# Four of six weight tiles in steps 2 to 8 of a chunk, two in an earlier pass, and a changed order of two loads

## The chip, the cores and the metric

The kernel runs on one core of a Trainium2 chip. The metric is the device time of one execution in microseconds, beginning to end. A core has TensorE (matmuls; PE in the profile, with its weight loads as PEld), VectorE (DVE), ScalarE (ACT), GpSimd (POOL) and SyncE (SP), which here issues every DMA. Each engine takes its instructions strictly in the order of the program; between engines, semaphores tell when data is there and when a buffer is free. SyncE too works in order: a DMA that has to wait holds up all DMAs behind it.

## What is computed

Two equal layers on an input of 2048 rows by 512 columns. Each adds a Fourier mixing and then an MLP block:

```python
def _A_ref(x, dft_seq_re, dft_seq_im, dft_hid_re, dft_hid_im):
    a = jnp.einsum("bsd,ed->bse", x, dft_hid_re)
    b = jnp.einsum("bsd,ed->bse", x, dft_hid_im)
    return jnp.einsum("ts,bse->bte", dft_seq_re, a) - jnp.einsum("ts,bse->bte", dft_seq_im, b)

def _B_ref(x, w1, w2, w3, w4):
    h = _gelu(_layernorm(x) @ w1)
    ...                                # h in four groups, shifted by +1, -1, +2, -2 rows
    x1 = x + hs @ w2
    return x1 + _gelu(_layernorm(x1) @ w3) @ w4

for _ in range(2):
    x = x + _A_ref(_layernorm(x), ...)
    x = x + _B_ref(_layernorm(x), ...)
```

w3 is 512 by 1376 and w4 1376 by 512. The same weights serve both layers.

## The kernel before

**Products in three parts.** Every f32 operand is split into a high part, rounded to the matmul's format, and a low part, the rest. A product is three matmuls (`mm3`, lines 301 to 303): high by high, high by low, low by high. The high part is a copy on ScalarE, the low part a subtraction on VectorE. Weights that come from HBM go through `raw` buffers and a ring of four blocks: line 247 writes a block's high half, line 264 its low half. The third matmul of an `mm3` group is the first that reads the low half of the left operand.

**The MLP by chunks.** The 2048 rows are four chunks of 512. The inner size of 1376 is cut into NF = 11 tiles of 128 (the last is padded). In layer 0, chunks 0 and 1 form the *first pair*, worked off by `by_pairs`; chunks 2 and 3 go one after the other through `mlp`. In layer 1 both pairs go through `by_pairs`, and the second of them is `last_pair`.

*`mlp`* runs 13 steps a chunk. Step t multiplies by tile t of w3 (12 matmuls, t < 11), takes the gelu (ScalarE, line 661) and splits it (VectorE, lines 667 and 664), and multiplies tile t - 2 by w4 (12 matmuls, t > 1). So steps 0, 1, 11 and 12 have 12 matmuls and the others 24. At its begin, step t prepares the low half of the ring block for step t + 2 and the high half of the one for t + 3. After each step the main loop (lines 1601 to 1621) adds other work for VectorE and ScalarE: in chunk 2 the w4 sums, in steps 9 and 10 the split of chunk 3's input (`rt_split`, lines 625 and 626), and from step 6 on, for the next layer's first product, the pieces called `xp`: statistics (line 315), normalisation (line 349), sums (lines 381 to 383), their high parts (lines 386 to 390) and low parts (line 401), for one pair of row tiles after another.

*`by_pairs`* multiplies a pair by w3 in five passes p = 0 to 4, one for two tiles, in the seven products of Strassen's scheme in Winograd's form (`prod`), with the additions (line 466) on VectorE. In each pass the two tiles of the pass before are multiplied by w4 for the pair's first chunk (`w4_part`, 12 matmuls a tile); two more follow after the last pass, then all eleven for the second chunk. The left operand of `w4_part` is an h block (a split gelu), of which four exist (`h4`). In layer 0, five to six points in every pass (`at_point`) carry preparatory work of `w_prep`: for p = 0 to 3 the sums, high and low parts of the next w3 tiles; in all passes the high and low parts of two w4 tiles (lines 929 and 933), which are written to HBM (`w4a`, line 934) and read again later (`w4r`, line 925). In pass 4 only the w4 tiles are left. The last thing that VectorE does for pass 4 is the low half of the h block that the second of the two late `w4_part` calls reads.

*The w4 sums.* `last_pair` multiplies by w4 in the same seven-product scheme, so it wants sums of blocks of w4. They are made once, in layer 0, for six tiles n = 0 to 5 (each a pair of w4's tiles; the sixth is half a one): `w4_raw` loads a tile (512 KB, three buffers), `w4_sums` makes four sums on VectorE (two for n = 5) and their high part on ScalarE (lines 800 and 804), `w4_lows` the low part on VectorE (line 808), and `w4_keep` writes the result to HBM (1 MB, lines 813 and 815). `w4_ahead` does this in chunk 2's `mlp`: sums of tile n after step 2n, lows after step 2n + 1, and there the load of tile n + 1; the write of tile n - 1 after step 2n. So tile 5's sums are behind step 10, and its lows behind step 11. The first load is issued just ahead of chunk 2.

*The end.* `last_pair` runs five passes of w3 products too, then seven passes over w4's sums (`steps`). `w4_in(i)` loads the weights of pass i in two DMAs or one; that for pass 0 stands at the begin of w3's pass 4, and it writes a buffer from which w3's pass 3 reads. `w4t_in` loads, in two DMAs of 512 KB, the blocks `w4t` that the last tile of a pass needs; it stands at the end of w3's pass 3.

Of the kernel before, what the change touches and what calls it, by code (L numbers as in the profile page):

```python
# [8 lines left out]
F32 = mybir.dt.float32  # L9
# [4 lines left out]
P = 128  # L14
# [5 lines left out]
CH = 512  # L20
# [23 lines left out]
def spectral_mlp_kernel(ctx: ExitStack, tc: tile.TileContext, x, ws, hs, w1, w2, w34, out, out_t):  # L44
# [42 lines left out]
    def at(name, word, *shape, dtype=F32R):  # L87
        return nc.alloc_sbuf_tensor_at(name, [P, *shape], dtype, offset=base + 4 * word).ap()

    def both(name, word, *shape):  # L90
        return at(name, word, *shape), at(name + "f", word, *shape, dtype=F32)
# [31 lines left out]
    extra = [at(f"extra{i}", EXT + i * D, D, dtype=F32) for i in range(6)]  # L123
    rest = [at(f"rest{i}", RAWS + i * D, D, dtype=F32) for i in range(8)]

    w4c, w4cf = zip(*(both(f"w4c{i}", word, 2, 4, 2 * P) for i, word in enumerate((W12, 3 * AY))))
    w4raw = [at(f"w4raw{i}", word, 2, CH, dtype=F32) for i, word in enumerate((STG, EXT, EXT + 2 * CH))]
    h_at = [XS + i * CH for i in range(4)] + [W12 + i * CH for i in range(NF + 4)]
    h_at += [ZW + i * CH for i in range(8)] + [RR + (8 + i) * CH for i in range(8)]
    hq = [at(f"hq{i}", word, CH, dtype=F32) for i, word in enumerate(h_at)]  # L130
# [651 lines left out]

    W4_UNITS = {"12": 0, "1": 1, "2": 2, "3": 3, "a11": (0, 0), "a12": (1, 0), "a22": (1, 1)}

    def w4_raw(n):
        to = w4raw[n % 3]
        if n < NF // 2:
            nc.sync.dma_start(to, w34[2 * n + LAG : 2 * n + LAG + 2, :, 1].rearrange("f p w -> p f w"))
        else:
            nc.sync.dma_start(to[:, 0], w34[NF - 1 + LAG, :, 1])  # L790

    def w4_sums(n):
        lo, w = w4cf[n % 2][:, 1], w4c[n % 2]
        (a11, a21), (a12, a22) = ([w4raw[n % 3][:, f, e * 2 * P : (e + 1) * 2 * P] for e in range(2)] for f in range(2))
        if n < NF // 2:
            add(lo[:, 1], a21, a22)
            add(lo[:, 3], a11, a21, ALU.subtract)
            add(lo[:, 2], lo[:, 1], a11, ALU.subtract)
            add(lo[:, 0], a12, lo[:, 2], ALU.subtract)
            nc.scalar.copy(w[:, 0], lo)  # L800
        else:
            add(lo[:, 0], a11, a21, ALU.subtract)
            add(lo[:, 1], a21, a11, ALU.subtract)
            nc.scalar.copy(w[:, 0, 0:2], lo[:, 0:2])

    def w4_lows(n):
        w, lo, u = w4c[n % 2], w4cf[n % 2][:, 1], slice(0, 4 if n < NF // 2 else 2)
        nc.vector.tensor_tensor(w[:, 1, u], lo[:, u], w[:, 0, u].bitcast(F32), op=ALU.subtract)

    def w4_keep(n):  # L810
        w = w4c[n % 2].bitcast(F32)
        if n < NF // 2:
            nc.sync.dma_start(w4s[:, n], w)
        else:
            nc.sync.dma_start(w4e, w[:, :, 0:2])

    def w4_ahead(t):

        n, odd = divmod(t, 2)
        if n > NF // 2:  # L820
            return
        if odd:
            w4_lows(n)
            if n < NF // 2:
                w4_raw(n + 1)
        else:
            if n:
                w4_keep(n - 1)
            w4_sums(n)

    def by_pairs(layer, zs, xin, dst):
        act = nc.scalar.copy
# [267 lines left out]
        def last_pair():  # L1100
# [90 lines left out]
            for p in range(NF // 2):  # L1191
                end = p == last - 1
                u, v, x, y = sets[p % 2]
                w = w3b[(5 + p) % 2]
                b1, b6, b5, b2, b7, b4, b3 = (bank() for _ in range(7))
                if end:
                    w4_in(0)
                prod(b1, w, 4, "11")
                nc.scalar.copy(u, b1)
                one_more()  # L1200
                prod(b6, w, 1, "t2")
                add(v, u, b6)
                prod(b5, w, 0, "t1")
                add(x, v, b5)
                sums(p - 1 if p else last)
                if end:
                    split_of(3)
                prod(b2, w, 5, "21")
                add(u, u, b2)
                gelu_to(("b11", p), u)  # L1210
                prod(b7, w, 2, "t3")
                add(v, v, b7)
                add(y, v, b5)
                gelu_to(("b22", p), y)
                one_more()
                if end:
                    split_of(4)
                    split_of(5)
                prod(b4, w, 6, "t4")
                add(v, v, b4)  # L1220
                gelu_to(("b21", p), v)
                prod(b3, w, 3, "22")
                add(x, x, b3)
                gelu_to(("b12", p), x)
                if p in (last - 3, last - 2):
                    split_of(p - last + 3)
                w3_load(5 + p + 2)
                if p == last - 2:
                    split_of(2)
                    w4t_in()  # L1230
            assert not todo
            sums(last - 1)

# [62 lines left out]
        for pair in range(n_pairs):  # L1296
# [36 lines left out]
            def w_prep(p):  # L1333

                n, i = p + 1, 2 * p + 2
                w4_lows = lambda: (w4_low(i), w4_low(i + 1))
                w4_highs = lambda: (w4_high(i), w4_high(i + 1))
                if n == NF // 2:
                    return {1: [w4_highs], 5: [w4_lows]}
                return {  # L1340
                    0: [lambda: w3_sums(n, 0), lambda: w3_highs(n, 1, 2)],
                    1: [lambda: w3_sums(n, 1), lambda: w3_highs(n, 0)],
                    2: [lambda: w3_lows(n, 1, 2), lambda: w3_load(n + 1)],
                    3: [w4_highs],
                    4: [lambda: w3_lows(n, 0), lambda: w3_keep(n)],
                    5: [w4_lows],
                }

# [54 lines left out]
            if layer == 0:  # L1403
                def more():
                    state.update(limit=w_items[1], load=len(pieces))
                    issue_dma()

                rt_in(2)
                bg += z3_last(scratch[0])
                bg += [lambda: (more(), rt_split(2, ((0, 2),))), lambda: rt_split(2, ((2, 4),)), *[lambda: ahead(1)] * 3]  # L1410
            for i in range(2):
# [31 lines left out]
    for layer in range(LAYERS):  # L1443
# [153 lines left out]
            break  # L1597

        tmps[:] = singles
        w4_raw(0)  # L1600
        for c in (2, 3):
            for t in mlp(c, acc4, mm4):
                if c == 2:
                    w4_ahead(t)
                    if t == STEPS - 1:
                        w4_keep(NF // 2)
                if c == 2 and t == 1:
                    rt_in(3)
                if c == 2 and t in (9, 10):
                    rt_split(3, ((2 * t - 18, 2 * t - 16),))  # L1610
                if c == 3 and t == 1:
                    for j in range(2 * TC, 3 * TC, 2):
                        rows(xs[j // 2], x2d, j, 2, False)
                n = STEPS * (c - 2) + t - 6
                if n >= 0:
                    if n == 0:
                        tmps[:] = [tmp[:, 4], tmp[:, 5]]
                    for k in range(6):
                        for step, f in enumerate(xp_stages):
                            if n == FIRST[k] + step:  # L1620
                                f(k)
# [57 lines left out]
```

## Time and profile before

| | us |
|---|---|
| Median of three runs | 1463.76 (1462.58 to 1463.79) |
| The profiled execution | 1462.0 |
| Its span, first to last instruction | 1460.0 |
| Granted clock of TensorE, mean over the span | 0.998 |
| The w4 sums' first load is issued, SP (line 788) | 621.49 |
| Last write of the w4 sums is issued, SP (line 815) | 690.33 |
| First matmul of chunk 2 in layer 0 | 618.71 |
| First matmul of `last_pair`'s passes over w4 | 1401.80 |

Time in the profile counts from the first instruction. A row of a timeline has the start, the length, the engine, the line in the kernel, the operation, out<-in by the names of the tiles (numbers of buffers left out), and in brackets how long the engine was idle before it, and what ended that. An instruction of VectorE or ScalarE that follows another of its engine can start before that one's end, since they overlap by some hundredths. The chain of waits is followed back from the last instruction: at each place it shows what the work there had waited for. A line like 466 is that of a helper (`add`), so the tile's name tells more than the line.

### The profile page before, as it was taken

Reading aid. Unit: us, or ns where it says so; the run is one execution under the profiler, and the core shown is the slowest. Engines: PE = TensorE matmul, PEld = TensorE weight load, DVE = VectorE, ACT = ScalarE, POOL = GpSimd, SP = SyncE. Lnnn points to the kernel's source line nnn. Section 1 sums busy time; section 2 is a strip of 40 time slices with the busy share of each in tenths; the row PEclk is TensorE's granted clock in tenths of the full one; section 3 lists DMA queues with packets and bytes.
Section 4 is the critical chain, followed back from the end, with each engine's and each line's share of the span. In section 5 each row is a group of like instructions: output and inputs, shape, how many; then the busy total and the mean of one; then the engine's idle time right before and its main releaser. Section 6 shows DMA issues by size and latency. Waiting matters only on the chain.

```text
span 1460.0 us, 17408 instructions
## 1 busy us (share of the span) xinstructions
PE 1446.3 (99%) x6344; PEld 1186.6 (81%) x6344; DVE 1170.9 (80%) x1643; ACT 730.9 (50%) x978; POOL 87.2 (6%) x111
## 2 busy tenths in 40 slices
PE   9999999999999999998999999999999999999998
PEld 8888888888888788886887888888888888888887
DVE  7876987988868896668989979979888688746686
ACT  5563454454556664335545534544545566433352
POOL 2100000000001000001100000000000010000000
PEclk9999999999999999999999999999999999999999
DMA  7336556556545767875435466565575458656594
GB/s 248 127 93 210 188 189 211 188 191 233 185 134 167 240 236 277 267 268 174 143 130 180 163 203 201 188 194 197 182 249 187 131 150 297 213 193 262 173 312 137
DMA packets 124806, 288.72 MB, mean 198 GB/s; under 512 B 8624, under 2 KB 50352, under 8 KB 122160
## 3 DMA queue, kind: packets, MB, share of 16 engines
q1 hardware_dynamic: 124720, 287.61, 59.6%
q8 instruction: 50, 0.82, 0.2%
q14 instruction: 36, 0.29, 0.1%
HBM read 234.88 MB, written 52.69 MB: 197 GB/s over the span
## 4 chain that ended last, share of the span: by engine, by line
PE 87%; DVE 7%; DMA 3%; ACT 1%; issue 1%; SPq 1%; DVEq 0%; POOL 0%; ACTq 0%; POOLq 0%
PE psd L301 10%; PE psd L303 10%; PE psd L302 10%; PE psa L301 8%; PE psa L303 8%; PE psa L302 8%; PE psc L303 6%; PE psc L301 6%; PE psc L302 6%; PE psb L303 6%; PE psb L301 6%; PE psb L302 5%; DVE ring L264 2%; DMA raw<-in_ws 1%; DMA w4u<-w4a 1%
## 5 line engine op out<-in xcount | busy, mean ns | idle before, releaser
L247 ACT CAST ring<-raw 128x1024 fp32r<-128x1024 f32 (+1 forms) x153 | 156.6, 1029 | 111.3 <-PE psd L303 51.3
L264 DVE TENSOR_TENSOR ring<-raw,ring 128x1024 fp32r<-128x1024 f32 (+1 forms) x154 | 181.9, 1185 | 28.0 <-ACT ring L247 26.7
L303 PE MATMUL psd<-ring,rr 128*128 128x512 f32 x208 | 80.9, 389 | 0.0
L302 PE MATMUL psd<-ring,rr 128*128 128x512 f32 x208 | 80.9, 389 | 0.0
L301 PE MATMUL psd<-ring,rr 128*128 128x512 f32 x208 | 80.9, 389 | 0.0
L341 POOL TENSOR_TENSOR rs<-ve,mhalf 128x4 f32<-128x4 f32 x16 | 27.8, 1738 | 611.4 <-DVE nm L340 611.4
L320 POOL TENSOR_TENSOR rs<-ve,mhalf 128x2 f32<-128x2 f32 (+1 forms) x33 | 33.4, 1014 | 413.7 <-DVE nb L319 405.9
L349 ACT ACTIVATE tmp<-xs,nb,rs 128x512 f32<-128x512 f32 x58 | 44.7, 809 | 15.4 <-POOL nb L321 15.4
L254 ACT CAST ring<-ring2f 128x1024 fp32r<-128x1024 f32 x28 | 29.6, 1056 | 44.0 <-DVE ring2f L253 44.0
L301 PE MATMUL psc<-ring,ay 128*128 128x512 f32 x128 | 49.9, 390 | 0.3 <-ACT rr11f L491 0.3
L302 PE MATMUL psc<-ring,ay 128*128 128x512 f32 x128 | 50.0, 391 | 0.0
L303 PE MATMUL psc<-ring,ay 128*128 128x512 f32 x128 | 49.8, 389 | 0.0
L303 PE MATMUL psb<-ring,ay 128*128 128x512 f32 x128 | 49.8, 389 | 0.0
L302 PE MATMUL psb<-ring,ay 128*128 128x512 f32 x128 | 49.8, 389 | 0.0
L301 PE MATMUL psb<-ring,ay 128*128 128x512 f32 x128 | 49.8, 389 | 0.0
L254 ACT CAST ring<-ring0f 128x1024 fp32r<-128x1024 f32 x28 | 29.6, 1057 | 40.1 <-DVE ring0f L253 40.1
L264 DVE TENSOR_TENSOR ring<-ring1f,ring 128x1024 fp32r<-128x1024 f32 (+1 forms) x50 | 49.1, 983 | 0.6 <-ACT ring L250 0.4
L264 DVE TENSOR_TENSOR ring<-ring3f,ring 128x1024 fp32r<-128x1024 f32 (+1 forms) x50 | 49.1, 983 | 0.2
L301 PE MATMUL psd<-ring,ay 128*128 128x512 f32 x126 | 49.0, 389 | 0.0
L302 PE MATMUL psd<-ring,ay 128*128 128x512 f32 x126 | 49.0, 389 | 0.0
L303 PE MATMUL psd<-ring,ay 128*128 128x512 f32 x126 | 49.0, 389 | 0.0
L302 PE MATMUL psa<-ring,ay 128*128 128x512 f32 x126 | 49.0, 389 | 0.0
(556 smaller groups left out, 4410.1 us busy)
## 6 DMA issues: line engine op xcount, KB each, us to landing
raw<-in_ws SPq DMA_DIRECT2D x183, 512.0 KB, 4.9
raw<-in_hs SPq DMA_DIRECT2D x56, 512.0 KB, 3.6
w3b<-w3d SPq DMA_DIRECT2D x10, 1792.0 KB, 7.4
w4r<-w4a SPq DMA_DIRECT2D x33, 512.0 KB, 4.5
raw<-in_w SPq DMA_DIRECT2D x26, 512.0 KB, 3.9
w3d<-w3b SPq DMA_DIRECT2D x5, 1792.0 KB, 6.7
x1d<-tmp SPq DMA_DIRECT2D x12, 512.0 KB, 6.3
xs<-x1d SPq DMA_DIRECT2D x12, 512.0 KB, 6.5
```

What stands on the lines that cost most here:

```text
L247: nc.scalar.copy(dest[:, a:b, 0], r[0][:, a:b])
L254: nc.scalar.copy(dest[:, :, 0], lo)
L264: nc.vector.tensor_tensor(lo[:, i], src[:, i], hi[:, i].bitcast(F32), op=ALU.subtract)
L301: nc.tensor.matmul(o, lh, rh, start=first, stop=False, skip_group_check=onto)
L302: nc.tensor.matmul(o, lh, rl, start=False, stop=False, skip_group_check=onto)
L303: nc.tensor.matmul(o, ll, rh, start=False, stop=last, skip_group_check=onto)
L320: nc.gpsimd.tensor_tensor(rs[:, :n], ve[:, :n], mhalf[:, 0, :n], op=ALU.pow)
L341: nc.gpsimd.tensor_tensor(rs, ve, mhalf[:, :, :2], op=ALU.pow)
L349: nc.scalar.activation(o, s, AF.Identity, bias=mr[2], scale=mr[1])
```

## The change

Names: `w4_raw`, `w4_sums`, `w4_lows` and `w4_keep` become `q4_raw`, `q4_sums`, `q4_lows` and `q4_keep`, with the same work.

Places in the first pair of layer 0: the load of tile 0 is issued at point 4 of pass 3, that of tile 1 at point 0 of pass 4. Sums and lows of tile 0 come at points 1 and 2 of pass 4, those of tile 1 at points 3 and 4. Tile 0's write stands at point 4, and tile 2's load at point 2; tile 1's write and tile 3's load follow the load of chunk 2's input behind the pass.

Places in chunk 2: tiles 2 to 5 are summed in steps 2, 4, 6 and 7, their lows follow in 3, 5, 7 and 8, and the last write is issued in step 9. Loads of tiles 4 and 5 are issued in steps 3 and 5.

Buffers: two for the loads instead of three, and the two work buffers lie elsewhere in SBUF.

In `last_pair`, `w4t_in` moves from the end of w3's pass 3 behind `w4_in(0)` at the begin of pass 4.

```diff
-    w4c, w4cf = zip(*(both(f"w4c{i}", word, 2, 4, 2 * P) for i, word in enumerate((W12, 3 * AY))))
-    w4raw = [at(f"w4raw{i}", word, 2, CH, dtype=F32) for i, word in enumerate((STG, EXT, EXT + 2 * CH))]
+    w4c, w4cf = zip(*(both(f"w4c{i}", word, 2, 4, 2 * P) for i, word in enumerate((EXT, 4 * CH))))
+    w4raw = [at(f"w4raw{i}", word, 2, CH, dtype=F32) for i, word in enumerate((STG, EXT + 4 * CH))]
...
-    def w4_ahead(t):
-
-        n, odd = divmod(t, 2)
-        if n > NF // 2:
-            return
-        if odd:
-            w4_lows(n)
-            if n < NF // 2:
-                w4_raw(n + 1)
-        else:
-            if n:
-                w4_keep(n - 1)
-            w4_sums(n)
+    QUADS = {
+        2: lambda: q4_sums(2),
+        3: lambda: (q4_lows(2), q4_raw(4)),
+        4: lambda: (q4_keep(2), q4_sums(3)),
+        5: lambda: (q4_lows(3), q4_raw(5)),
+        6: lambda: (q4_keep(3), q4_sums(4)),
+        7: lambda: (q4_lows(4), q4_sums(5)),
+        8: lambda: (q4_keep(4), q4_lows(5)),
+        9: lambda: q4_keep(5),
+    }
...
                 if end:
                     w4_in(0)
+                    w4t_in()
                 prod(b1, w, 4, "11")
...
                 if p == last - 2:
                     split_of(2)
-                    w4t_in()
...
                 if n == NF // 2:
-                    return {1: [w4_highs], 5: [w4_lows]}
+                    return {
+                        0: [lambda: q4_raw(1)],
+                        1: [w4_highs, lambda: q4_sums(0)],
+                        2: [lambda: q4_lows(0), lambda: q4_raw(2)],
+                        3: [lambda: q4_sums(1)],
+                        4: [lambda: q4_keep(0), lambda: q4_lows(1)],
+                        5: [w4_lows],
+                    }
...
-                    4: [lambda: w3_lows(n, 0), lambda: w3_keep(n)],
+                    4: [lambda: w3_lows(n, 0), lambda: w3_keep(n), *[lambda: q4_raw(0)] * (n == NF // 2 - 1)],
...
                 rt_in(2)
+                q4_keep(1)
+                q4_raw(3)
                 bg += z3_last(scratch[0])
...
-        w4_raw(0)
         for c in (2, 3):
             for t in mlp(c, acc4, mm4):
                 if c == 2:
-                    w4_ahead(t)
-                    if t == STEPS - 1:
-                        w4_keep(NF // 2)
+                    QUADS.get(t, lambda: None)()
```

More of the change, by code (lines that the diff above doesn't have):

```diff
@@ L783, in spectral_mlp_kernel, with q4_raw @@
     W4_UNITS = {"12": 0, "1": 1, "2": 2, "3": 3, "a11": (0, 0), "a12": (1, 0), "a22": (1, 1)}
-    def w4_raw(n):
-        to = w4raw[n % 3]
+    def q4_raw(n):
+        to = w4raw[n % 2]
         if n < NF // 2:
@@ L790, in w4_raw, with q4_sums @@
             nc.sync.dma_start(to[:, 0], w34[NF - 1 + LAG, :, 1])
-    def w4_sums(n):
+    def q4_sums(n):
         lo, w = w4cf[n % 2][:, 1], w4c[n % 2]
-        (a11, a21), (a12, a22) = ([w4raw[n % 3][:, f, e * 2 * P : (e + 1) * 2 * P] for e in range(2)] for f in range(2))
+        (a11, a21), (a12, a22) = ([w4raw[n % 2][:, f, e * 2 * P : (e + 1) * 2 * P] for e in range(2)] for f in range(2))
         if n < NF // 2:
@@ L804, in w4_sums, with q4_lows, q4_keep @@
             nc.scalar.copy(w[:, 0, 0:2], lo[:, 0:2])
-    def w4_lows(n):
+    def q4_lows(n):
         w, lo, u = w4c[n % 2], w4cf[n % 2][:, 1], slice(0, 4 if n < NF // 2 else 2)
         nc.vector.tensor_tensor(w[:, 1, u], lo[:, u], w[:, 0, u].bitcast(F32), op=ALU.subtract)
-    def w4_keep(n):
+    def q4_keep(n):
         w = w4c[n % 2].bitcast(F32)
```

## The prediction

> **What bounds the kernel now.** I read the page's busy times first, then TensorE's waits, then its timeline where those waits are, then the chain of waits there.
>
> ```profile
> PE 1446.3 (99%) x6344; PEld 1186.6 (81%) x6344; DVE 1170.9 (80%) x1643; ACT 730.9 (50%) x978; POOL 87.2 (6%) x111
> ```
> ```profile
> PE psc L303 <- DVE ring L264: 3.5, 1, 3.5
> PE psd L301 <- DVE h L667: 1.7, 1, 1.7
> ...
> PE psd L303 <- DMA w4u<-w4a: 0.8, 1, 0.8
> ...
> PE psb L303 <- DVE ring L264: 0.3, 1, 0.3
> ```
>
> TensorE is busy for 99% of the span, so a change gains only what TensorE waits. Four waits matter here. Three lie in the third chunk of the first layer's MLP and the start of the fourth; one lies near the end. The timeline of TensorE gives their places, and the windows give the clock (columns: window, us, then busy us and count of PE, PEld, DVE, ACT, POOL, granted clock, DMA share, GB/s).
>
> ```profile
> 618.71 0.39 PE L301 MATMUL psc<-rt,ring 128*128 128x512 f32 x1
> ...
> 624.15 0.39 PE L301 MATMUL psb<-rt,ring 128*128 128x512 f32 x1
> ...
> 680.52 0.63 PE L301 MATMUL psa<-ring,h 128*128 128x512 f32 x1
> 680.94 0.63 PE L302 MATMUL psa<-ring,h 128*128 128x512 f32 x1
> ...
> 689.98 0.79 PE L303 MATMUL psc<-rt,ring 128*128 128x512 f32 x1 [3.50 <-DVE ring L264]
> ...
> 699.85 0.50 PE L303 MATMUL psb<-rt,ring 128*128 128x512 f32 x1
> ```
> ```profile
> 676.00:695.00 19.00, 13.70 (x44) 10.11 (x43) 16.67 (x35) 12.51 (x18) 3.05 (x4) 0.82 0.56 168
> ...
> 720.00:750.00 30.00, 30.00 (x134) 24.86 (x133) 23.65 (x42) 12.71 (x19) 2.16 (x2) 1.00 0.32 104
> ```
>
> From 618.71 to 624.15 there are 24 matmuls: 0.2267 us each. The third matmul of the fourth chunk's step 3 starts at 699.85. Before it lie 24 (steps 0, 1), 216 (2 to 10), 24 (11, 12), 24 (0, 1 of the next chunk), 24 (2) and 2: 314 matmuls, 71.2 us. They took 81.1, so **9.9 us are lost in this stretch**: the waits of 0.3, 1.7 and 3.5 us, some tenths of refill behind each, and about 3.2 us at a slow clock. From 680.52 to 680.94 is 0.42 us, nearly twice 0.2267, and the granted clock of 676 to 695 is 0.82. Some eight matmuls run so behind each of the two long waits, at 0.2 us extra each: 1.6 us per wait.
>
> **The third chunk, term one.** The chain of waits shows what made VectorE late; of VectorE's timeline I add a first and a last row.
>
> ```profile
> 668.02 1.51 ACT tmp L349 x2
> ...
> 670.05 0.50 ACT tmp L661
> 670.57 0.44 DVE h L667
> ...
> 671.79 1.14 DVE w4c L808
> ...
> 677.95 0.35 DVE h L667
> ...
> 679.00 0.76 DVE w4c1f L466 x2
> 679.78 0.62 ACT w4c L804
> ...
> 681.38 1.23 DVE rt L626
> ...
> 683.21 0.60 DVE w4c L808
> ...
> 687.55 1.20 DVE st L315 x2
> ```
> ```profile
> 622.26 0.43 DVE L667 CAST h<-tmp 128x512 fp32r<-128x512 f32 x1 [1.23 <-ACT tmp L661]
> ...
> 698.58 1.22 DVE L264 TENSOR_TENSOR ring<-raw,ring 128x1024 fp32r<-128x1024 f32 x1
> ```
>
> Today tiles 4 and 5 are summed in steps 8 and 10, and their lows follow in 9 and 11, just where the next layer's sums and statistics begin. With the change, lows of tile 5 in step 8 are the last.
>
> Step by step. (1) Without a wait, TensorE ends the first half of step 9 after 24+168+12 = 204 matmuls: 618.71 + 46.25 = 664.96. In step 0 VectorE's cast came 0.83 us after such an end (621.43 to 622.26), so step 9's comes at 665.8 instead of 670.57. ScalarE then no longer waits, in step 8, for tile 4's sums before its two normalisations (668.02) and the gelu (670.05). (2) From 670.57 to 677.95 VectorE works without a gap; 1.14 of these 7.38 us are tile 4's lows, which move: step 10's cast comes at 665.8 + 6.24 = 672.0. (3) From 677.95 to 687.55 are 9.60 us; out go the two adds of tile 5 (0.76), its lows (0.60) and the 1.6 us from the adds' end to 681.38, in which VectorE waited for ScalarE's rt cast behind the copy of tile 5 (679.78). The statistics begin at 672.0 + 6.6 = 678.6. (4) From there to the end of the ring subtraction (698.58 + 1.22 = 699.80) are 12.25 us; none of it changes: 690.9.
>
> So the matmul of 699.85 starts at about 691.0: **8.8 us earlier**. TensorE alone would be there at 618.71 + 71.2 = 689.9, so 1.1 us of wait stay, now on work of the next layer. Steps 2 to 7 hold the moved tiles: a tile is 1.47 us of sums and 1.14 of lows on VectorE beside 2.3 us of ring and h work (1.22 + 0.43 + 0.69 for a whole block), in steps of 24 matmuls, 5.44 us, so they fit; step 7 (lows and two adds, 1.9 us) is the fullest, with two steps of reserve before its ring block is read. The first tile no longer waits for a load begun in the chunk, so the wait of 0.3 us at 630 goes too. Afterwards VectorE stands to TensorE as before, and at 720 to 750 it is busy for 23.65 of 30 us, so the gain should carry. Bounds of this term: 9.9 (nothing waits) and 8.8 - 1.6 = 7.2 (the left wait is followed by a slow clock).
>
> **The first pair's last pass, term two.** Two tiles move into pass p = 4.
>
> ```profile
> 570.55 0.69 DVE L466 TENSOR_TENSOR rest<-rest,psa 128x512 f32<-128x512 f32 x1 [1.41 <-PE psa L303]
> ...
> 583.57 0.69 DVE L664 TENSOR_TENSOR h<-tmp,h 128x512 fp32r<-128x512 f32 x1
> ```
> ```profile
> 585.87 0.39 PE L303 MATMUL psc<-w4r,h 128*128 128x512 f32 x1
> ```
> ```profile
> 636.35 0.75 DVE L466 TENSOR_TENSOR w4c1f<-w4raw 128x256 f32<-128x256 f32 x2
> ...
> 637.82 1.22 DVE L264 TENSOR_TENSOR ring<-raw,ring 128x1024 fp32r<-128x1024 f32 x1
> ```
> ```profile
> L800 ACT CAST w4c<-w4c0f x3: 1053/1054/1055, 629.4 to 667.1; 128x1024 fp32r<-128x1024 f32 x3
> ```
> ```profile
> 533.00:548.00 15.00, 15.00 (x68) 12.36 (x67) 13.68 (x24) 8.82 (x15) 0.00 (x0) 1.00 0.92 319
> ...
> 563.00:579.00 16.00, 16.00 (x71) 13.11 (x70) 8.96 (x14) 6.02 (x10) 0.00 (x0) 1.00 0.71 252
> ```
> ```profile
> L925 SPq DMA_DIRECT2D w4r<-w4a x2: 372/802/1231, 563.3 to 566.0; - x2
> L934 SPq DMA_DIRECT2D w4a<-w4r x2: 860/1042/1223, 563.7 to 564.7; - x2
> ...
> DMA to landing us min/median/max: 7.6/9.1/10.1
> ```
>
> By volume it fits: 5.2 us on VectorE and 2.1 on ScalarE, where 563 to 579 has 7.0 and 10.0 us free, and an earlier pass ran 13.68 of 15 us without holding TensorE. By order it is tight. The low half of the last gelu (583.57, ending 584.26) is read at 585.87: 1.6 us of reserve. Tile 0 (sums from 571.15, copy until 573.8, lows until 575.0) delays the additions by at most half a microsecond. Tile 1's sums can start at 576.9, its copy ends at 579.5, its lows at 580.7; then follow the two w4 lows (1.2), two lows of h (1.2) and the addition of the fourth product at 583.1 instead of 581.5. The low half then ends at about 585.85: the reserve is used up exactly, at no cost.
>
> What decides is tile 1's load. It is issued behind the four DMAs of 563.3 to 566.0, which land 7.6 to 10.1 us after issue; the last lands at about 575.6. Ahead now lies the load of tile 0 too. Of 563 to 579, 252 GB/s at a share of 0.71 make 355 GB/s at full share, so each 512 KB takes 1.5 us: tile 1's data lands at about 578.6, an estimate. VectorE waits 1.7 us in front of everything queued behind these sums, and TensorE waits for h as long: **1.7 us lost**. Bounds: 0 (data there by 576.9; nothing in this pass had a wait to remove, so not below nothing) and 3.3 (a slow clock behind it). Later DMAs (2 MB written, 1 MB loaded) are hidden: a w4r load has five tiles of 12 matmuls, 2.7 us each, ahead of its use. SP issues the kept tile's write, and behind it the next w4r load, up to 4 us later, inside that reserve.
>
> **The last pair, term three.** From the chain of waits and TensorE's timeline:
>
> ```profile
> 1394.65 8.54 DMA w4u<-w4a
> ```
> ```profile
> 1392.28 0.39 PE L301 MATMUL psa<-b,w3b 128*128 128x512 f32 x1
> ...
> 1403.24 0.50 PE L303 MATMUL psd<-hs,w4u 128*128 128x512 f32 x1 [0.80 <-DMA w4u<-w4a]
> ...
> 1409.72 0.39 PE L301 MATMUL psd<-hs,w4t 128*128 128x512 f32 x1
> ```
>
> The two w4t loads (1 MB) go behind the first pass's weights. These can't be issued before 1392.28, when the pass that reads their buffer has ended; that is 2 us ahead of 1394.65, and 1 MB less stands in the queue before them. The wait of 0.8 us and its refill go: **1.0 us gained** (bounds 0 and 1.1). What is late next is w4t: issued at about 1394, at worst 8.54 us to land, 1402.6, read at about 1408.7.
>
> **Sum**: 8.8 + 1.0 - 1.7 = 8.1 us. The profiled execution took 1462.0 us (span 1460.0), 1.8 under the median of the three runs; it becomes 1453.9 and the median of 1463.76 becomes **1455.7**.
>
> **Rivals.** *Both new places stay clear*: tile 1's load lands in time and the next layer's work fits. 9.9 + 1.1 = 11.0 gained, 1452.8. For it: 13.68 busy of 15 us did no harm. Against it: step (4). *A slow clock behind what stays*: waits of 1.1 and 1.7 us may be long enough. For it: a wait of 1.7 us was followed by the stretch at 680. Against it: none of the waits under 1 us was. One stretch gives 1457.3, both 1458.9. [...] *The change doesn't do what it says*: VectorE's lateness is the next layer's, and only the removed instructions count (1.14 + 0.76 + 0.60 = 2.5 us): 2.5 + 1.0 - 1.7 = 1.8 gained, 1462.0. Against it: the 1.6 us of waiting, and the 4.8 us of step (1), hang on the tiles. *Slower*: tile 1's load is so late that h holds TensorE. From 576.9 on each microsecond costs one; 9.8 us of gain are used up, with the slow clock's 1.6, from a landing at 585 on, and at 588.5 the median is 1467.2. It would need 21 us to land, against 10.1 at most in these rows.
>
> **Chances.** Forecast 0.45, slow clock 0.25, both clear 0.14, not what it says 0.10, slower 0.06. The first three lie within 1452.4 to 1459.5: that is the range, 0.84. About 0.2%, 2.9 us, is what a measurement of this kernel can tell from no change: faster 0.84, same 0.11, slower 0.05.
>
> **What would show it.** Right: no wait of TensorE between 620 and 685; step 9's cast near 666 after allowing for the shift ahead of the chunk; a wait of about 1 us on a ring block in the next chunk's step 3; a wait of 1 to 2 us on h behind p = 4, with w4raw named as what VectorE waited for; no wait on w4u, none on w4t. Wrong: a wait on a ring block or h within steps 9 to 12, a w4r load that TensorE waits for, or a slow clock where no wait is left.

## The result, and the profile after

| | before | changed |
|---|---|---|
| Median of the runs beside each other | 1463.17 us (four runs, 1461.61 to 1463.79) | 1454.44 us (four runs, 1454.05 to 1456.33) |
| Ratio, 95% interval | | 0.9946 (0.9934 to 0.9958) |
| Span of the profiled execution | 1460.0 | 1452.0 |

The medians differ by 8.7 us, the spans by 8.0; 8.1 were forecast, with a median of 1455.7. On another chip the changed kernel took 1455.18 us against 1462.40, ratio 0.9948 (0.9936 to 0.9960).

The busy times and TensorE's waits of the changed kernel (engine, tile, line, what it waited for; total, times, longest in us):

```profile
PE 1442.7 (99%) x6344; PEld 1184.3 (82%) x6344; DVE 1171.0 (81%) x1643; ACT 731.9 (50%) x978; POOL 87.2 (6%) x111
```
```profile
PE psc L301 <- ACT h L674: 0.9, 1, 0.9
...
PE psb L303 <- DVE ring L264: 0.6, 1, 0.6
PE psc L302 <- DVE w4r L930: 0.5, 1, 0.5
```

The work is the same: VectorE is busy for 1171.0 us as against 1170.9. What went is waiting: of the waits of 3.5, 1.7, 0.8 and 0.3 us none is left. Three new ones stand in their place, 0.9, 0.6 and 0.5 us. TensorE's timeline shows them at their places:

```profile
582.54 0.39 PE L301 MATMUL psc<-w4r,h 128*128 128x512 f32 x1
583.39 0.50 PE L302 MATMUL psc<-w4r,h 128*128 128x512 f32 x1 [0.47 <-DVE w4r L930]
...
587.11 0.50 PE L301 MATMUL psc<-w4r,h 128*128 128x512 f32 x1 [0.93 <-ACT h L674]
...
620.83 0.39 PE L301 MATMUL psc<-rt,ring 128*128 128x512 f32 x1
...
693.14 0.50 PE L303 MATMUL psb<-rt,ring 128*128 128x512 f32 x1 [0.62 <-DVE ring L264]
...
1395.02 0.39 PE L301 MATMUL psd<-hs,w4u 128*128 128x512 f32 x1
...
1395.47 0.39 PE L303 MATMUL psd<-hs,w4u 128*128 128x512 f32 x1
...
1401.82 0.39 PE L301 MATMUL psd<-hs,w4t 128*128 128x512 f32 x1
```
```profile
676.00:695.00 19.00, 18.32 (x80) 14.51 (x79) 18.44 (x33) 12.98 (x19) 1.36 (x2) 1.00 0.37 110
```

Five places tell the account; the last matmul of the kernel closes it:

| Start of | before | changed | gained so far |
|---|---|---|---|
| a product of pass p = 4, 200 matmuls ahead of the third chunk | 572.56 | 572.40 | 0.16 |
| the third chunk | 618.71 | 620.83 | -2.12 |
| the third matmul of the next chunk's step 3 | 699.85 | 693.14 | 6.71 |
| the first matmul on w4u | 1401.80 | 1395.02 | 6.78 |
| the third one | 1403.24 | 1395.47 | 7.77 |
| the last matmul | 1455.73 | 1447.83 | 7.90 |

So pass p = 4 lost 2.28 us (forecast 1.7), the chunk gained **8.83** (8.8), the last pair 0.99 (1.0). These are 7.54 in all; the other 0.36 of the 7.90 lie outside the three places (0.16 ahead of them, 0.07 and 0.13 behind). In the window of 676 to 695 the granted clock is 1.00 where it was 0.82.

### The profile page after: what moved, and what is told of

Read it like the earlier page. It is cut to its first block, busy times and chain, and to the rows that moved or that the text cites. A ratio compares the mean times of both kernels' runs of the same rounds, so it can differ in the third digit from the quotient of the medians.

```text
span 1452.0 us, 17408 instructions
## 1 busy us (share of the span) xinstructions
PE 1442.7 (99%) x6344; PEld 1184.3 (82%) x6344; DVE 1171.0 (81%) x1643; ACT 731.9 (50%) x978; POOL 87.2 (6%) x111
## 4 chain that ended last, share of the span: by engine, by line
PE 91%; DVE 5%; DMA 1%; ACT 1%; issue 1%; SPq 0%; POOL 0%; DVEq 0%; ACTq 0%; POOLq 0%
PE psd L303 10%; PE psd L301 10%; PE psd L302 10%; PE psa L301 8%; PE psa L303 8%; PE psa L302 8%; PE psc L303 6%; PE psc L301 6%; PE psc L302 6%; PE psb L303 6%; PE psb L301 6%; PE psb L302 6%; DMA w4raw<-in_w 1%; DVE ring L264 1%; DMA zt1f<-zd 1%
## 5 line engine op out<-in xcount | busy, mean ns | idle before, releaser
L301 PE MATMUL psd<-ring,ay 128*128 128x512 f32 x126 | 49.0, 389 | 0.0
L303 PE MATMUL psd<-ring,ay 128*128 128x512 f32 x126 | 49.0, 389 | 0.0
L301 PE MATMUL psa<-ring,ay 128*128 128x512 f32 x126 | 49.0, 389 | 0.0
L302 PE MATMUL psa<-ring,ay 128*128 128x512 f32 x126 | 49.0, 389 | 0.0
```

The source lines that it names most:

```text
L301: nc.tensor.matmul(o, lh, rh, start=first, stop=False, skip_group_check=onto)
L302: nc.tensor.matmul(o, lh, rl, start=False, stop=False, skip_group_check=onto)
L303: nc.tensor.matmul(o, ll, rh, start=False, stop=last, skip_group_check=onto)
```

## The experiments

All are read by two distances, which don't depend on what came before: **A**, from that product of p = 4 to the chunk's start (46.15 before, 48.43 changed), and **B**, from there to the third matmul of the next chunk's step 3 (81.14 before, 72.31 changed). Where an edit adds a line, the line numbers of later lines are one or more higher. "Ratio" is to the kernel before, on the same chip.

| Kernel | A | B | median, us | ratio, 95% interval |
|---|---|---|---|---|
| tile 1's load early | 47.15 | 72.29 | 1453.02 | 0.9936 (0.9922 to 0.9949) |
| both loads early | 46.33 | 72.29 | 1452.13 | 0.9925 (0.9912 to 0.9939) |
| w4 low halves first | 47.44 | 72.28 | 1453.87 | 0.9940 (0.9927 to 0.9954) |
| tiles 4 and 5 late | 48.50 | 77.61 | 1460.63 | 0.9987 (0.9978 to 0.9996) |
| tile 5 late | 48.64 | 75.30 | 1457.47 | 0.9965 (0.9952 to 0.9979) |
| tile 4 late | 48.31 | 74.21 | 1456.46 | 0.9961 (0.9946 to 0.9976) |
| no tiles in the chunk | 48.53 | 72.28 | 1453.93 | 0.9946 (0.9931 to 0.9961) |
| six tiles, steps 2 to 8 | 46.15 | 75.24 | 1455.38 | 0.9950 (0.9938 to 0.9963) |
| before, first load early | 46.15 | 78.09 | 1458.87 | 0.9972 (0.9961 to 0.9983) |
| before, end only | 46.16 | 80.95 | 1461.46 | 0.9993 (0.9984 to 1.0002) |
| both loads early, next layer later | 46.36 | 71.50 | 1453.02 | 0.9937 (0.9925 to 0.9950) |
| changed, again | 48.50 | 72.29 | 1455.18 | 0.9948 (0.9936 to 0.9960) |

For the same order of work, A lies between 48.31 and 48.64 us in the six kernels with the changed pass p = 4 and between 46.15 and 46.16 in those with the old one; B lies between 72.28 and 72.31 with the changed chunk, and is 81.14 and 80.95 with the old one. So the traces tell apart what the medians, which are uncertain by some 2 us, can't.

### What costs 2.3 us in pass p = 4

VectorE's rows of the changed kernel there, and rows of its chain of waits (start, length, what):

```profile
572.11 0.76 DVE L466 TENSOR_TENSOR w4c0f<-w4raw 128x256 f32<-128x256 f32 x2 [1.03 <-DMA w4raw<-in_w]
...
577.25 0.68 DVE L664 TENSOR_TENSOR h<-tmp,h 128x512 fp32r<-128x512 f32 x1
578.79 0.76 DVE L466 TENSOR_TENSOR w4c1f<-w4raw 128x256 f32<-128x256 f32 x2 [0.86 <-DMA w4raw<-in_w]
...
581.51 1.23 DVE L808 TENSOR_TENSOR w4c<-w4c1f,w4c 128x1024 fp32r<-128x1024 f32 x1 [1.17 <-ACT w4c L800]
582.65 0.68 DVE L930 TENSOR_TENSOR w4r<-w4r4f,w4r 128x512 fp32r<-128x512 f32 x1
583.26 0.68 DVE L930 TENSOR_TENSOR w4r<-w4r5f,w4r 128x512 fp32r<-128x512 f32 x1
583.86 1.29 DVE L664 TENSOR_TENSOR h<-hc,h 128x512 fp32r<-128x512 f32 x2
585.06 0.68 DVE L466 TENSOR_TENSOR rest<-rest,psa 128x512 f32<-128x512 f32 x1
...
587.09 0.69 DVE L664 TENSOR_TENSOR h<-tmp,h 128x512 fp32r<-128x512 f32 x1 [0.75 <-ACT h L674]
```
```profile
568.05 10.71 DMA w4raw<-in_w
578.79 1.11 DVE w4c1f L466 x3
...
580.43 1.06 ACT w4c L800
...
582.65 1.29 DVE w4r L930 x2
...
586.44 0.63 ACT h L674
587.11 0.50 PE psc L301
```

VectorE waits 1.03 us for tile 0's load and 0.86 us for tile 1's. The chain runs from tile 1's load through the sums, ScalarE's copy and the lows to the low halves of two w4 tiles, and on to h, which TensorE reads at 587.11. The second matmul of the first late `w4_part` reads one of those w4 halves (583.39). It would have started at 582.77, 0.12 us after that subtraction began. This wait of TensorE's isn't on the chain.

**Tile 1's load early.**

```diff
+    w4raw = [w4raw[0], tmp[:, 0:2], *w4raw * 2]
...
-        to = w4raw[n % 2]
+        to = w4raw[n]
...
-                        0: [lambda: q4_raw(1)],
...
-                    4: [lambda: w3_lows(n, 0), lambda: w3_keep(n), *[lambda: q4_raw(0)] * (n == NF // 2 - 1)],
+                    4: [lambda: w3_lows(n, 0), lambda: w3_keep(n), *[lambda: q4_raw(0), lambda: q4_raw(1)] * (n == NF // 2 - 1)],
```


> The changed kernel with only the load of w4's second pair of tiles (tile 1) moved: issued right behind tile 0's load at the end of pass p = 3, into a buffer of its own, instead of at the start of p = 4. In the changed kernel it was issued at 568.05 and landed at 578.76, VectorE waited 0.86 us for it, and TensorE lost 2.3 us in p = 4 (0.6 on the low half of a w4 tile, some 1.4 with refill on h, the rest in refills). Theory 'order behind a full VectorE': the load is only 0.86 us of it. VectorE's wait goes and everything behind it comes 0.86 us earlier: the low half of the w4 tile is then in time (0.6 gone), but h comes at 586.2 for a TensorE that is there at 585.4, so about 1.2 of the 2.3 us stay; the third chunk starts at 619.7 instead of 620.8, and the time is about 1453.3. Rival 'the landing is all' (the prediction's term two: nothing is lost if the data is there by 576.9): both waits go, the chunk starts at 618.5, and the time is 1452.1. Rival 'the load does not matter': 620.8 and 1454.4.

A is 47.15: 1.00 us above what it was before the change, where 1.2 were expected, so 1.28 of the 2.28 us are gone. VectorE no longer waits for this load, and TensorE no longer for the low half of the w4 tile; a wait on h stays:

```profile
585.95 0.50 PE L302 MATMUL psc<-w4r,h 128*128 128x512 f32 x1 [0.43 <-ACT h L675]
```

So tile 1's landing isn't all: tile 0's load, for which VectorE waits at 572.11 in the changed kernel, is still late here (a wait of 0.71 us).

**Both loads early.** As above, but both at point 2 of pass p = 3:

```diff
-                    2: [lambda: w3_lows(n, 1, 2), lambda: w3_load(n + 1)],
+                    2: [lambda: w3_lows(n, 1, 2), lambda: w3_load(n + 1), *[lambda: q4_raw(0), lambda: q4_raw(1)] * (n == NF // 2 - 1)],
...
-                    4: [lambda: w3_lows(n, 0), lambda: w3_keep(n), *[lambda: q4_raw(0)] * (n == NF // 2 - 1)],
+                    4: [lambda: w3_lows(n, 0), lambda: w3_keep(n)],
```


> The changed kernel with the loads of tiles 0 and 1 both issued two points earlier, in pass p = 3 behind the lows of the last w3 tile that read the staging buffer (tile 1 into a buffer of its own). Theory 'order behind a full VectorE': tile 0's sums no longer wait 1.03 us either, so the whole chain of VectorE in p = 4 starts that much earlier, tile 1's sums start near 576.9, h is there at about 585.2 for a TensorE that comes at 585.4: all of the 2.3 us go, the third chunk starts at 618.5, time about 1452.1 us. Rival 'the copies and lows of the two tiles alone are too much for this pass, whenever their data come': a wait on h of 0.5 to 1 us stays, chunk start 619.2 to 619.8, time 1453.0 to 1453.6. Rival 'the earlier loads only push back the four DMAs of 563 to 566': a w4r load is waited for and nothing is gained, 1454.4 or more.

A is 46.33, 0.18 above before. The windows of 563 to 590 of the changed kernel and of this one (columns: us, then busy us of PE, PEld, DVE, ACT, POOL, clock, DMA share, GB/s):

```profile
563.00:590.00 27.00, 25.60 (x109) 20.04 (x108) 17.97 (x31) 10.84 (x17) 0.00 (x0) 1.00 0.92 329
```
```profile
563.00:590.00 27.00, 27.00 (x119) 21.87 (x118) 19.83 (x34) 11.46 (x18) 0.00 (x0) 1.00 0.92 329
```

TensorE is busy throughout, at the same load of the DMA engines. Tile 1's sums start at 576.11, 4.33 us behind the product from which A is counted, without a wait. So the pass has room for both tiles when the data of both is there, and no w4r load is late.

**The w4 low halves first.**

```diff
-                        3: [lambda: q4_sums(1)],
+                        3: [w4_lows, lambda: q4_sums(1)],
...
-                        5: [w4_lows],
```


> The changed kernel with the two w4 low halves of the last pass issued ahead of tile 1's sums instead of behind its lows; the loads stay where they are. Theory 'a reader was missed: the first late w4 product waits for the low half of its w4 tile, which stands on VectorE behind tile 1': the low halves now fill VectorE's 0.86 us of waiting for tile 1's load, TensorE's wait on w4r (0.6 us with refill) goes, and what stands behind comes about 0.8 us earlier; a wait on h of about 0.9 us stays, so about 1.2 of the 2.3 us stay, the chunk starts at 619.7, time about 1453.3 us. Rival 'only the landing of tile 1 counts': the wait on w4r turns into as much more wait on h, chunk start 620.8, 1454.4.

A is 47.44, 1.29 above before. The wait on w4r is gone with the loads where they were:

```profile
577.34 0.68 DVE L930 TENSOR_TENSOR w4r<-w4r4f,w4r 128x512 fp32r<-128x512 f32 x1
577.94 0.69 DVE L930 TENSOR_TENSOR w4r<-w4r5f,w4r 128x512 fp32r<-128x512 f32 x1
578.54 0.75 DVE L466 TENSOR_TENSOR w4c1f<-w4raw 128x256 f32<-128x256 f32 x2
```
```profile
585.65 0.50 PE L301 MATMUL psc<-w4r,h 128*128 128x512 f32 x1 [0.70 <-ACT h L674]
```

The two subtractions fill what was a wait for the load, and the sums begin without one; h is ready about a microsecond earlier. So the order on VectorE, too, sets the loss. That TensorE no longer waits on w4r isn't what gains here; the part on the prediction shows why.

### What the chunk gained: place or amount

**Tiles 4 and 5 late.** The old steps and, for them, the old result buffers, here and in the next two runs:

```diff
...
-        6: lambda: (q4_keep(3), q4_sums(4)),
-        7: lambda: (q4_lows(4), q4_sums(5)),
-        8: lambda: (q4_keep(4), q4_lows(5)),
-        9: lambda: q4_keep(5),
+        6: lambda: q4_keep(3),
+        8: lambda: q4_sums(4),
+        9: lambda: q4_lows(4),
+        10: lambda: (q4_keep(4), q4_sums(5)),
+        11: lambda: q4_lows(5),
+        12: lambda: q4_keep(5),
```


> The changed kernel with the last two pairs of tiles of the third chunk put back to where they were before (sums in steps 8 and 10, lows in 9 and 11, kept in 10 and 12), with the old buffers for them; tiles 0 to 3 stay as changed, so the chunk still holds four tiles. Theory 'place': what was gained in the chunk is that VectorE is clear of tiles when the next layer's sums and statistics begin. Then most of it is lost again: tile 4's lows (1.14 us) are back ahead of step 10's cast, tile 5's adds and lows and ScalarE's copy (0.76 + 0.60 + 1.6) ahead of the statistics and the ring block, VectorE's rest before these is less, and TensorE waits about 4 us on a ring block in the next chunk with some 1.6 us of slow clock behind: 4.9 us more, 1459.3 us (4 to 6.5 more). Rival 'amount': two tiles fewer in the chunk are what counts; the loss stays under 1 us, 1454.4 to 1455.4.

B is 77.61: 5.30 of the 8.83 us are lost again, with as many tiles in the chunk. Place it is, for this part.

**Tile 5 late** (tile 4 in steps 6 and 7):

```diff
...
-        7: lambda: (q4_lows(4), q4_sums(5)),
-        8: lambda: (q4_keep(4), q4_lows(5)),
-        9: lambda: q4_keep(5),
+        7: lambda: q4_lows(4),
+        8: lambda: q4_keep(4),
+        10: lambda: q4_sums(5),
+        11: lambda: q4_lows(5),
+        12: lambda: q4_keep(5),
```


> The changed kernel with tile 5 alone back at its old place (sums in step 10, lows in 11, kept in 12), tiles 4 and 5 with their old result buffers; tile 4 stays in steps 6 and 7. With tiles 4 and 5 both back the stretch from the chunk's start to the third matmul of the next chunk's step 3 took 77.61 us, changed 72.31. Theory (step 3 of the prediction: two adds 0.76, lows 0.60, and 1.6 us in which VectorE waits for ScalarE behind the copy of this tile): tile 5 alone costs about 3 of the 5.3 us: a ring wait of about 2.3 us more, and a slow clock behind it; 75.0 to 75.8 us, time 1457.1 to 1457.9. Rival 'steps 1 and 2 are what counts' (tile 4 ahead of the casts of steps 9 and 10): tile 5 alone costs under 1.4 us; 72.3 to 73.7. Rival 'tile 5 is all of it': 77 us or more.

B is 75.30, 2.99 more. VectorE's rows show the three pieces: two adds, the wait of 1.64 us, the lows.

```profile
675.35 0.75 DVE L466 TENSOR_TENSOR w4c5f<-w4raw 128x256 f32<-128x256 f32 x2
677.75 1.23 DVE L626 TENSOR_TENSOR rt<-rt1f,rt 128x1024 fp32r<-128x1024 f32 x1 [1.64 <-ACT rt L625]
...
679.49 0.69 DVE L808 TENSOR_TENSOR w4c<-w4c5f,w4c 128x512 fp32r<-128x512 f32 x1
```
```profile
686.34 0.50 PE L303 MATMUL psc<-rt,ring 128*128 128x512 f32 x1 [2.23 <-DVE ring L264]
```

**Tile 4 late** (tile 5 ahead of it, its load in step 4 in place of 5):

```diff
...
-        6: lambda: (q4_keep(3), q4_sums(4)),
-        7: lambda: (q4_lows(4), q4_sums(5)),
-        8: lambda: (q4_keep(4), q4_lows(5)),
-        9: lambda: q4_keep(5),
+        6: lambda: (q4_keep(3), q4_sums(5)),
+        7: lambda: q4_lows(5),
+        8: lambda: (q4_keep(5), q4_sums(4)),
+        9: lambda: q4_lows(4),
+        10: lambda: q4_keep(4),
```


> The changed kernel with tile 4 alone back at its old place (sums in step 8, lows in 9, kept in 10); tile 5 (the half tile) goes ahead of it, in steps 6 and 7. From the chunk's start to the third matmul of the next chunk's step 3: 72.31 us changed, 75.30 with tile 5 late, 77.61 with both late. Theory (steps 1 and 2 of the prediction: the cast of step 9 behind tile 4's sums and ScalarE's copy, its lows of 1.14 us ahead of step 10's cast): VectorE comes to the statistics 1 to 2 us later, less than with tile 5, since it was ahead of TensorE there; 73.7 to 74.7 us, time about 1456.3 us. Rival 'each tile costs its share, 5.3 in all': 74.6 and no wait on h. Rival 'only what stands behind step 10 counts': 72.3 to 73.2.

B is 74.21, 1.90 more. Counted from the chunk's start, step 9's cast comes at 47.92 in place of 47.13, step 10's at 55.22 in place of 53.30: between the two lie 1.13 us more, the lows. So 0.79 + 1.13 make up the 1.90. No matmul waits on h. Each tile costs what its place does; 1.90 + 2.99 are 4.89 of the 5.30, and 0.36 of the rest arise, with both late, between the casts of steps 9 and 10. The result buffers aren't the cause: the tile that stays early has its old one too in these two runs, and with tile 5 late step 9's cast comes at 47.12, as in the changed kernel.

**No tiles in the chunk.**

```diff
-        2: lambda: q4_sums(2),
-        3: lambda: (q4_lows(2), q4_raw(4)),
-        4: lambda: (q4_keep(2), q4_sums(3)),
+        4: lambda: q4_keep(2),
...
```


> The changed kernel with the loads, sums, copies and lows of the four tiles in the third chunk left out (their four writes stay and write what the buffers hold, so the sums of w4's tiles 2 to 5 are not computed). Changed kernel: 72.31 us from the chunk's start to the third matmul of the next chunk's step 3, of which 1.1 us are gaps just ahead of that matmul (0.22 and 0.77, and 0.1 of refill). Theory (the prediction's end of term one): what is left there is work of the next layer; without any tile it stays, 72.2 to 72.4, the wait on the ring block 0.5 to 0.8 us. Rival 'the tiles still hold it': the waits go, 71.2 us, time about 1453.3 us.

B is 72.28 with the same wait as in the changed kernel. The four tiles cost TensorE nothing where they stand now; what waits there waits for the next layer's work.

**Six tiles in steps 2 to 8.**

```diff
...
+        2: lambda: (q4_sums(0), q4_raw(2), q4_raw(3)),
+        3: lambda: (q4_lows(0), q4_sums(1), q4_raw(4), q4_raw(5)),
+        4: lambda: (q4_keep(0), q4_lows(1), q4_sums(2)),
...
+        8: lambda: (q4_keep(4), q4_lows(5)),
```


> The changed kernel with nothing of the tiles in pass p = 4: all six pairs of tiles are summed in the third chunk, as before, but one in each of the steps 2 to 7, the last lows in step 8, with four load buffers and three result buffers, and tiles 0 and 1 loaded ahead of the chunk. Distance from the same matmul of p = 4 (200 matmuls ahead of the chunk) to the chunk's start: 46.15 us before, 48.43 changed; from the chunk's start to the third matmul of the next chunk's step 3: 81.14 before, 72.31 changed. Theory 'place': VectorE has to be clear of tiles by step 8, however many there are. Then the first distance is 46.2 again (2.3 us won back) and the second one grows by about 2 us to 74.3, because VectorE is about full in steps 2 to 8; time 1454.1 us. Rival 'amount': what the chunk gained is two tiles fewer. Then the second distance is 78 to 81 and the time 1458 to 1461. Rival 'result buffers': VectorE waits for the writing out of a tile three before, with waits of TensorE on ring blocks in steps 6 to 9.

A is 46.15: what p = 4 lost comes back. B grows by 2.93, to 75.24, a microsecond more than expected, but far from 78. In all the two tiles in p = 4 are worth 0.65 us more there than in the chunk, less than the medians can tell.

**Before, with the first load early.** This run came out of a surprise. With tiles 4 and 5 late, step 9's cast came at 47.91 from the chunk's start; before, at 51.86. VectorE had been late long before tile 4. Its timeline before has this row:

```profile
627.78 0.76 DVE L466 TENSOR_TENSOR w4c0f<-w4raw 128x256 f32<-128x256 f32 x2 [4.37 <-DMA w4raw<-in_w]
```
```diff
                 rt_in(2)
+                w4_raw(0)
...
-        w4_raw(0)
         for c in (2, 3):
```


> The kernel before with one edit: the load of the first pair of w4's tiles is issued at the end of the first pair, behind the rt load, and not in step 1 of the third chunk; all six tiles stay in the chunk at their old steps. In the kernel before VectorE waited 4.37 us for this load (issued 621.49, landed 627.76) and 1.21 us for that of tile 2, and its casts were 4 to 7 us behind those of the changed kernel from step 2 on; from the chunk's start to the third matmul of the next chunk's step 3 it took 81.14 us, with four tiles of which the last two stand at their old places 77.61. Theory 'the first load made VectorE late, and it never caught up': both waits go, the casts up to step 8 are on time (step 9's cast 47.9 us from the chunk's start in place of 51.86), tiles 4 and 5 cost what they cost there; 77.4 to 78.0 us, time about 1459 us. Rival 'two tiles fewer': the six tiles fill VectorE whatever the load; 80.3 to 81.1 us, the cast at 51 or later, time 1461.5 or more. Between them, 78.5 to 80: both have a part.

B is 78.09, 3.05 less than before, and the time goes from 1463.90 to 1458.87. Step 9's cast comes at 48.80. VectorE's waits are now smaller ones on later loads:

```profile
633.36 0.76 DVE L466 TENSOR_TENSOR w4c1f<-w4raw 128x256 f32<-128x256 f32 x2 [1.61 <-DMA w4raw<-in_w]
643.00 0.76 DVE L466 TENSOR_TENSOR w4c0f<-w4raw 128x256 f32<-128x256 f32 x2 [0.91 <-DMA w4raw<-in_w]
```

The figure lies 0.09 us outside the first theory's range, and the casts aren't on time up to step 8 (that of step 3 comes at 18.99 from the chunk's start, not at 14.42 as with tiles 4 and 5 late): VectorE catches up, but not wholly. So the 8.83 us have parts: **3.05** the first load, **0.48** (78.09 to 77.61) the two tiles fewer together with these loads, **5.30** the place of tiles 4 and 5. The parts hold in this order only: with every tile in steps 2 to 8, two tiles more cost 2.93 us (75.24 against 72.31).

### The last pair

**Before, end only.**

```diff
                 if end:
                     w4_in(0)
+                    w4t_in()
...
                     split_of(2)
-                    w4t_in()
```


> The kernel before with only the third part of the change: the two w4t loads are issued behind the first pass's weights in the last pair. Theory (term three): the third matmul on w4u comes 0.45 us after the first instead of 1.44, the wait of 0.80 us on w4u is gone, no wait on w4t appears, and nothing else moves: 1.0 us faster in the trace, less than such a measurement can tell from no change (ratio 0.9993). Rival 'the wait moves to w4t': w4t lands after it is read, 8 us later, and the 1.0 us is given back there.

The third matmul on w4u comes 0.45 us after the first, in place of 1.44, and no matmul waits on w4t:

```profile
1401.12 0.39 PE L301 MATMUL psd<-hs,w4u 128*128 128x512 f32 x1
...
1401.57 0.39 PE L303 MATMUL psd<-hs,w4u 128*128 128x512 f32 x1
```

The medians can't tell this from no change, as expected.

### Both loads early, and the next layer later

```diff
-FIRST, X6, X7 = (1, 3, 5, 8, 11, 13), 2, 4
+FIRST, X6, X7 = (1, 3, 6, 8, 11, 13), 2, 4
```


> Both loads of tiles 0 and 1 early, as in the run with both early (distance of p = 4 46.3 us), and the third pair of row tiles of the next layer taken one step later (its statistics, normalisation, sums, high and low parts each start one step later; 6 in place of 5 in the list of first steps). Theory 'what is left at the chunk's end is the next layer's work alone': the sums of that pair (1.8 us) no longer stand ahead of the ring block of the next chunk's step 3, the wait on it (0.77 us with refill) goes; 71.2 to 71.6 us from the chunk's start to that matmul in place of 72.31, no new wait in steps 4 to 8; time 1451.3 us against 1452.1. Rival 'VectorE is behind whatever the order': the wait comes a step later, about as long; 1452.1.

At both places it did what was expected: A 46.36, B 71.50, no wait on the ring block. The time didn't follow: 1453.02. In the profiled execution a wait stands elsewhere, on a block of the second layer:

```profile
1098.79 1.23 DVE L254 TENSOR_TENSOR ring3f<-raw,raw 128x1024 f32<-128x1024 f32 x1 [3.14 <-DMA raw<-in_ws]
...
1101.21 0.50 PE L303 MATMUL psc<-ring,ay 128*128 128x512 f32 x1 [1.35 <-DVE ring L265]
```

The changed kernel, run again, has 1.76 us there for VectorE and no wait of TensorE's. VectorE waits for this load in every trace here, 1.56 to 3.14 us, the longest being this one; TensorE then waits for the block in three other kernels too, 0.52 us with both loads early, 0.33 with tile 4 late and 0.20 with tiles 4 and 5 late. What makes the load later here wasn't tried.

> The changed kernel once more, on the chip of the other two runs, to compare them with it. 1454.4 us, ratio to the kernel before 0.9946 again; the gaps of p = 4 (0.62 and 1.09) and of the next chunk's step 3 (0.77) as in the first profile if they are set by the order of work, and others by several tenths if they are chance.

The gaps were 0.72 and 1.08 in p = 4 and 0.72 on the ring block, within 0.1 us of the first profile: the order of work sets them. In the other kernels with the same pass the first of them is between 0.52 and 0.88 us.

The best that was run is *both loads early*, at 1452.13 us. Its ratio, 0.9925 (0.9912 to 0.9939), lies below the changed kernel's 0.9946 and 0.9948, though the intervals overlap.

## Why the prediction was right, and where not

**Reading.** That the stretch of the third chunk loses 9.9 us held: 1.1 are left now. That its slow clock was part of the loss did not. The next point shows it.

**Term one, 8.8 against 8.83.** The forecast places, put on the old start of the chunk, came true within 0.1 us: step 10's cast at 672.0 (53.30 from the start is 672.01), the statistics at 678.6 (678.63), the ring block's end at 690.9 (690.97). Behind it is a plain rule that the prediction used and the runs confirm: in every kernel that has the same order behind these statistics, B is their start plus about 12.4 us.

| | statistics, from the chunk's start | B | B less statistics |
|---|---|---|---|
| before | 68.76 | 81.14 | 12.38 |
| changed | 59.92 | 72.31 | 12.39 |
| tiles 4 and 5 late | 65.18 | 77.61 | 12.43 |
| tile 5 late | 62.89 | 75.30 | 12.41 |
| tile 4 late | 61.83 | 74.21 | 12.38 |
| six tiles | 62.86 | 75.24 | 12.38 |
| before, first load early | 65.70 | 78.09 | 12.39 |

VectorE sets the end of this stretch. Some of these kernels have no slow stretch there, some one, the kernel before two; it makes no difference. Slow matmuls only shortened the wait behind them.

- *Step (1), size right, cause mostly wrong.* The cast of step 9 was to gain 4.8 us because ScalarE no longer waits for tile 4's sums; it gained 4.73. But tile 4 at its old place makes this cast only 0.79 us late (47.92 against 47.13). The larger part was inherited: VectorE's 4.37 us of waiting for the first load, which the prediction booked as 0.3 us, because it looked at TensorE's wait only. The size came out because the new time was worked out from TensorE's pace, not from the cause.
- *Steps (2) and (3), right.* 1.14 us for tile 4's lows were 1.13; 0.76 + 0.60 + 1.6 for tile 5 were 2.99.
- *Step (4), right.* 1.1 us of gaps stay (0.22 and 0.77, and 0.11 of refill between, that is, in matmuls that take longer just behind a wait: 0.34 us from 686.79 to 687.13 in place of 0.227), and they wait for the next layer's work: without any tile they stay as well.

**Term two, 1.7 against 2.28: the term that was mis-sized.** The reader that sets the loss was named rightly: the low half of the last h, which TensorE reads, unhindered, 13.31 us behind the product from which A is counted (585.87 less 572.56). The wait at 587.11 names its high half, which is ready 0.72 us earlier; the low half holds TensorE again two matmuls later.

| | low half of h ready, from that product | late by | wait on w4r ahead of it | A less 46.15 | A's loss less lateness |
|---|---|---|---|---|---|
| changed | 15.38 | 2.07 | 0.62 | 2.28 | 0.21 |
| changed, again | 15.48 | 2.17 | 0.72 | 2.35 | 0.18 |
| tile 5 late | 15.64 | 2.33 | 0.88 | 2.49 | 0.16 |
| tile 4 late | 15.27 | 1.96 | 0.52 | 2.16 | 0.20 |
| w4 low halves first | 14.39 | 1.08 | none | 1.29 | 0.21 |
| tile 1's load early | 14.12 | 0.81 | none | 1.00 | 0.19 |
| both loads early | 13.32 | 0.01 | none | 0.18 | 0.17 |

The loss is h's lateness and about 0.2 us, whether TensorE waits on w4r before it or not. So the prediction passed over a reader, the first late w4 product, but that cost nothing of its own: without the wait on w4r TensorE would have come to h earlier and waited there.

- *What was mis-sized.* The forecast puts h's low half at 585.85 + 1.7, 14.99 us behind the product; it was ready at 15.38. Of these 0.39 us, 0.35 are the load: tile 1's sums start on it 6.39 us behind the product in place of 6.04 (at 578.79 in place of 578.6, while TensorE itself was 0.16 us ahead). The 0.2 us lost beside the lateness, mostly refill, are not in the term.
- *What failed: tile 0's load.* The prediction has tile 0's sums begin at 571.15, as if the data were there by then; they waited for it until 572.11. So VectorE came to tile 1's sums at 577.9, not at 576.9, and waited for that load 0.86 us, not 1.7. As tile 1's load came last, the size hardly suffered. The bound of 0 ("data there by 576.9") did fail: with that load early it lands at about 573.1, and 1.00 us stays. The bound comes nearly true when both loads are early: tile 1's sums start 4.33 us behind the product, where the forecast had 4.34, and 0.18 us are lost.

**Term three, right:** 0.99 against 1.0. w4t was read at 1401.82 without a wait.

**The rivals.** *Not what it says* fell: the place of tiles 4 and 5 alone is worth 5.30 us where it allowed 2.5. *Slow clock*: behind the waits of 0.9 and 0.6 us the clock stayed at 1.00. What a slow stretch behind the second of them would have cost, no run shows. *Slower* needed a landing at 585. *Both clear* didn't happen; *both loads early, next layer later* has both places clear in its trace.

**The sum.** That 8.1 lies so close to the 7.9 in the trace is in part luck: term two's loss was 0.58 us too small, and 0.36 us were gained outside the three places, of which the prediction has nothing.

## What to carry to other kernels

When an in-order engine is late, look for its first long wait, not for the work beside the place where the bottleneck finally waits: 4.37 us of VectorE's waiting in one step of the chunk showed up as 0.3 us on TensorE there, and as 3 us at the chunk's end. When work is put ahead of a queue, time every load that it waits for, not only the last one (here 1.03 us for tile 0's and 0.86 for tile 1's). A wait of the bottleneck that stands ahead of a longer one costs nothing by itself if nothing that the longer one waits for hangs on it (here 0.52 to 0.88 us on w4r: with this wait or without it, the loss was h's lateness and about 0.2 us): look for the reader that is late last. And when two engines take turns at being late, a delay on the one that waits anyway costs nothing (here, with two slow stretches of TensorE, one or none, it was 12.38 to 12.43 us from the statistics to the end of B); settle first which of them sets the end of the stretch.

## What was not expected of the hardware

The length of a wait alone doesn't tell whether the clock drops. Between the starts of two matmuls lay 2.12 us in the kernel before (676.22 to 678.34), and matmuls from 680.1 to 683.1 came at 0.427 us; the same order of work in *end only* left 1.88 us (676.49 to 678.37), and six tiles left 2.49 us (681.91 to 684.40), both with the clock at 1.00 behind them (678.40 to 681.80 and 684.40 to 687.80). With tile 5 late, 2.62 us (683.72 to 686.34) had a slow stretch behind them: matmuls at 0.427 us from 687.0 to 690.0. The windows of before and of the six tiles (columns as above, clock third from the right):

```profile
675.00:678.40 3.40, 1.67 (x9) 1.05 (x7) 3.19 (x11) 0.00 (x0) 1.03 (x1) 1.00 0.00 0
...
680.00:683.40 3.40, 3.40 (x10) 2.58 (x9) 2.02 (x3) 3.37 (x6) 0.00 (x0) 0.54 0.89 353
```
```profile
681.00:684.40 3.40, 1.30 (x7) 0.75 (x5) 3.29 (x11) 1.97 (x3) 0.67 (x1) 1.00 0.03 11
684.40:687.80 3.40, 3.01 (x12) 2.17 (x12) 3.40 (x5) 2.59 (x4) 0.70 (x2) 1.00 0.56 154
```

In the kernel before, no gap between the chunk's start and the stretch at 680 is longer than those 2.12 us. Why a gap of 2.12 us has slow matmuls behind it and one of 2.49 has none, these runs don't show.
